# The load of q split into 120 and 8 partitions, in an attention kernel with routed adapters

## The chip, the cores and the metric

The kernel runs on one core of one Trainium2 chip. The metric is device time in microseconds; smaller is better. The core has five engines that run their own queues of instructions: PE (TensorE, matrix products), DVE (VectorE), ACT (ScalarE), POOL (GpSimd) and SP (SyncE). Here SP issues nearly all transfers, and 16 DMA engines carry them out.

## What is computed

There are 4 batches of 8 heads with 768 positions of 64 values. Each position of q and k is hashed into a bucket by the signs of six projections. Attention is allowed only between positions of the same bucket. The result, brought to 3072 rows of 512, goes through a small mixture of adapters: each row takes its two best of eight experts, each of rank 16, and adds what they give.

```python
q_bits = (np.einsum('bhsd,dk->bhsk', q, proj) > 0)
k_bits = (np.einsum('bhsd,dk->bhsk', k, proj) > 0)
mask = q_bucket[:, :, :, None] == k_bucket[:, :, None, :]
scores = np.where(mask, scale * np.matmul(q, k.transpose(0, 1, 3, 2)), -1e9)
attn = softmax(scores)
x = (attn @ v) as (B * S, H * D)
logits = x @ w_gate                     # top 2 of 8, softmax over them
out = x + sum over the two experts e of w_e * (x @ A[e]) @ B[e]
```

## The kernel before

The work is cut into 16 pairs of heads (`N`, counted from 0). A pair has six slots. In each slot PE computes one stretch of scores, 128 x 1536, into one of two buffers (`score`, line 265), and ACT takes the exponential of it (line 286); 96 such exponentials are the backbone of the run. The rest of each slot is other work for earlier and later pairs, written out by hand in `work` (line 691). Every engine runs its list in exactly that order.

What is done for one pair p, and when:

- **Loads.** `loadqk` (line 144) loads q (i = 0) or k (i = 1) of a pair, both heads at once: 128 partitions, two runs of 384 floats in each, 384 KB. From pair 2 on, pair p issues q of pair p + 4 in slot 2, directly ahead of v of pair p + 2 (`loadv`), and k of pair p + 4 in slot 4. The tiles `nat` have four buffers. The first loads are issued in `start` (pairs 0 to 2), `first` (pairs 3 and 4) and pair 1's slots.
- **Hashing.** `turn32` (line 175, instruction on line 180) transposes q or k of one head in blocks of 32 on DVE, `hash` multiplies with the projections on PE, `sign` (line 205) makes signs `sg` on DVE, `signs_out` (line 212) stores them to DRAM as `dr`, and `signs_in` (lines 220 and 224) loads them back in another order, into rows 64 to 71 of `aug`. A bucket match thereby becomes part of the score's matrix product.
- **q and k for the scores.** `natcast` (line 232) casts `nat` to bf16 on POOL. q goes through PE (`trq`) and DVE (`qcopy`, line 247) into `aug`; k of most pairs goes through a transposing transfer (`turnk`, line 253). `shift` (line 261) copies the second head's half on POOL.
- **After the scores.** `pvk` (line 303) multiplies with v on PE, `norm` (lines 321 and 323) divides on DVE and writes `x`, `to_bf` (line 332) casts on POOL to `xb`, and `turn` (line 338) transposes it by a transfer into `xT`.
- **Adapters.** In some pairs, called routing pairs here, `lgz`, `route1`, `route_exp`, `gates` (lines 434 and 436) compute the routing and `zm` for three tiles, and `zt_dma` (line 489) transposes `zm` by a transfer into `zT`. In the pair behind, `delta` multiplies on PE (`dl`, line 503) and adds on DVE (`acc`, line 524), and `store` writes to the output (line 533).

In the steady part SP therefore issues for each pair, in this order: q, v, the store of signs (dr), xT, in routing pairs zT, k, in some pairs output stores, the signs' load (aug<-dr), and k's transpose (aug<-nb). An issue that has to wait holds up all that stand behind it on SP. SP's and ACT's transfers share eight completion semaphores in turn, so an issue also waits until the transfer eight issues before it has landed.

The readers of the q part of `nat` are `turn32` on DVE, two for each pair, and `natcast` on POOL, one for each pair.

Of the kernel before, what the change touches and what calls it, by code (L numbers as in the profile page):

```python
# [19 lines left out]
class Emitter:  # L20
# [123 lines left out]
    def loadqk(self, p, i, h=None, eng=None):  # L144
        if p >= self.N:
            return
        eng = eng or self.nc.sync
        if p not in self.nat:
            self.nat[p] = self.natp.tile([self.P, 2, 2, self.T * self.D], F32, tag="nat", name=f"nat{p}")
        s = self.src((self.q, self.k)[i], p)  # L150
        if h is None:
            eng.dma_start(out=self.nat[p][:, i], in_=s)
        else:
            eng.dma_start(out=self.nat[p][:, i, h], in_=s[:, h])
# [811 lines left out]
```

## Time and profile before

| | us |
|---|---|
| median of 3 runs | 167.91 |
| the three runs | 171.59, 167.91, 166.63 |
| the profiled execution | 167.42 |
| its span, first to last instruction | 165.6 |

The span is 1.8 us shorter than the execution's own time. The views quoted below are of this one execution. In the table of engines a name is followed by busy time, share of the span and number of instructions; PEld is PE's loading of weights, which overlaps its products. The slices cut the span into 40 equal parts with the busy share in tenths. In the groups and waits an arrow points from what was awaited to who waited. In a timeline a line has its start, its length, the engine, the line of the kernel, the operation, the tiles as out<-in, and in brackets the idle time before it with what ended it. In the chain of waits the columns are start, length and what the chain went through; a name such as SPq is the issuing queue of an engine. The granted clock of PE was 0.986 on average.

### The profile page before, as it was taken

How to read it: one execution, taken by the hardware profiler on the slowest of the kernel's cores; microseconds unless marked ns; L12 is line 12 of the kernel's file. 1: busy time of each engine (PE TensorE's matmuls, PEld its weight loads, DVE VectorE, ACT ScalarE, POOL GpSimd, SP SyncE). 2: the span in 40 equal slices, each digit the busy share in tenths (PEclk: the TensorE clock that was granted, in tenths of full speed). 3: DMA queues.
4: the chain of work that ended last, by engine and by line, in shares of the span. 5: the costliest groups of instructions: out<-in, count | busy, mean ns of one | idle time of the engine just before them, and what ended most of it. 6: DMA issues, size and time to landing. Idle time of an engine off the chain costs nothing.

```text
span 165.6 us, 5300 instructions
## 1 busy us (share of the span) xinstructions
PE 149.5 (90%) x2148; PEld 101.8 (61%) x2148; DVE 110.4 (67%) x290; ACT 143.6 (87%) x122; POOL 110.4 (67%) x164
## 2 busy tenths in 40 slices
PE   6787998997999999999998999899999999999840
PEld 2244675675666666666765677576756666879500
DVE  5786895554747699486858696659766545656770
ACT  3466989798999999899998999989999999998640
POOL 3688969696878879694979397948976742510060
PEclk9999999999999999999999999999999999999995
DMA  5874659999999999999989999999998950439036
GB/s 146 279 246 117 199 125 205 260 237 224 169 202 190 211 190 241 185 214 340 256 178 254 321 255 155 251 247 285 174 245 153 248 94 4 86 124 294 6 132 248
DMA packets 58331, 33.09 MB, mean 200 GB/s; under 512 B 43714, under 2 KB 56002, under 8 KB 58306
## 3 DMA queue, kind: packets, MB, share of 16 engines
q1 hardware_dynamic: 57632, 32.46, 89.0%
q8 instruction: 17, 0.28, 0.7%
q10 hardware_dynamic: 674, 0.29, 0.6%
q14 instruction: 8, 0.07, 0.2%
HBM read 20.18 MB, written 7.05 MB: 164 GB/s over the span
## 4 chain that ended last, share of the span: by engine, by line
PE 49%; DMA 20%; DVE 16%; POOL 4%; issue 3%; SPq 3%; ACT 1%; DVEq 1%; POOLq 0%
PE s L283 21%; DMA nat<-in_k_dram 13%; PE pv L303 11%; DMA aug<-dr 5%; PE hs L193 4%; DVE R L180 3%; DVE acc L524 3%; PE pv L291 2%; DMA dr<-sg 2%; DVE x L323 2%; PE dl L503 2%; PE tr L241 2%; PE lz L405 2%; DVE gw L434 2%; DVE zm L436 1%
## 5 line engine op out<-in xcount | busy, mean ns | idle before, releaser
L286 ACT ACTIVATE P<-s 128x1536 bf16<-128x1536 f32 x96 | 135.3, 1450 | 11.3 <-PE s L283 9.0
L283 PE MATMUL s<-aug 71*128 71x512 bf16 (+2 forms) x432 | 78.5, 308 | 4.2 <-DMA aug<-dr 3.0
L283 PEld LDWEIGHTS <-aug 71*128 71x128 bf16 x432 | 34.2, 97 | 25.6 <-issue 8.0
L303 PEld LDWEIGHTS <-P 128*128 128x128 bf16 x1080 | 41.7, 98 | 7.2
L303 PE MATMUL pv<-vb,P 128*128 128x65 bf16 x1080 | 44.3, 193 | 0.0
L180 DVE STREAM_TRANSPOSE R<-nat 128x384 f32<-128x384 f32 x62 | 33.3, 560 | 5.8 <-DMA nat<-in_k_dram 4.9
L261 POOL COPY aug<-aug 64x768 bf16<-64x768 bf16 x30 | 24.8, 827 | 16.3 <-issue 11.1
L232 POOL CAST nb<-nat 128x768 bf16<-128x768 f32 x30 | 24.8, 828 | 2.0 <-DMA nat<-in_q_dram 0.7
L332 POOL CAST xb<-x 128x768 bf16<-128x768 f32 x15 | 12.4, 824 | 15.1 <-issue 6.5
L247 DVE TENSOR_SCALAR aug<-tr 128x768 bf16<-128x768 bf16 x20 | 11.0, 555 | 14.5 <-issue 6.5
L323 DVE TENSOR_TENSOR x<-pv,ri 128x384 f32<-128x384 f32 x30 | 16.7, 557 | 1.0
L170 POOL TENSOR_TENSOR vs<-vn 128x384 f32<-128x384 f32 x16 | 15.9, 996 | 0.0
L193 PE MATMUL hs<-R,hst 128*32 128x192 f32 x248 | 15.4, 332 | 0.2 <-DVE R L180 0.2
L524 DVE SCALAR_TENSOR_TENSOR acc<-dl,rt,x 128x512 f32<-128x512 f32 x18 | 13.3, 738 | 1.6 <-PE dl L503 1.6
L168 POOL CAST vb<-vn 128x768 bf16<-128x768 f32 x16 | 13.3, 828 | 0.2 <-DMA vn<-in_v_dram 0.2
L205 DVE TENSOR_SCALAR sg<-hs,ssc 128x192 bf16<-128x192 f32 (+1 forms) x17 | 7.1, 418 | 8.4 <-PE hs L193 8.4
L193 PEld LDWEIGHTS hs<-R,hst 128*32 128x32 f32 x248 | 7.2, 109 | 7.7 <-issue 2.5
L321 DVE RECIPROCAL ri<-pv 128x6 f32<-128x6 f32 x30 | 5.5, 184 | 9.4 <-PE pv L303 9.4
L291 PE MATMUL pv<-vb,eps 128*128 128x390 bf16 x30 | 10.1, 337 | 1.2 <-DVE x L323 0.6
L241 PE MATMUL tr<-ident_bf,nb 128*128 128x128 bf16 x120 | 10.0, 219 | 0.0
L241 PEld LDWEIGHTS <-nb 128*128 128x128 bf16 x120 | 8.4, 97 | 2.6
L522 POOL TENSOR_TENSOR acc<-acc,x 128x512 f32<-128x512 f32 x2 | 2.5, 1266 | 9.8 <-ACT acc L521 9.8
(111 smaller groups left out, 107.0 us busy)
## 6 DMA issues: line engine op xcount, KB each, us to landing
vn<-in_v_dram SPq DMA_DIRECT2D x16, 384.0 KB, 6.3
nat<-in_q_dram SPq DMA_DIRECT2D x15, 384.0 KB, 5.2
nat<-in_k_dram SPq DMA_DIRECT2D x15, 384.0 KB, 5.1
out_dram<-acc SPq DMA_DIRECT2D x7, 512.0 KB, 3.5
out_dram<-acc SPq DMA_DIRECT2D x9, 256.0 KB
dr<-sg SPq DMA_DIRECT2D x14, 48.0 KB, 5.0
aug<-dr SPq DMA_DIRECT2D x14, 48.0 KB
nat<-in_q_dram SPq DMA_DIRECT2D x2, 192.0 KB
```

The lines of the kernel that those rows point to most:

```text
L170: nc.gpsimd.tensor_add(out=s3, in0=vn[:, :, 0:3, :], in1=vn[:, :, 3:6, :])
L180: self.nc.vector.transpose(out=self.R[p][:, i, h, :], in_=self.nat[p][:, i, h, :])
L193: nc.tensor.matmul(out=hs[32 * j:32 * j + 32], lhsT=self.hst[:, hf].rearrange("p b i -> p (b i)"), rhs=rhs, start=(hf == 0), stop=(hf == 1 ...
L232: self.nc.gpsimd.tensor_copy(out=self.nb[p][:, i].rearrange("p t h d -> p h t d"), in_=self.nat[p][:, i].rearrange("p h (t d) -> p h t d", ...
L241: self.nc.tensor.transpose(out=tr[:, t, :], in_=self.nb[p][:, i, t].rearrange("p h d -> p (h d)"), identity=self.ident_bf)
L261: self.nc.gpsimd.tensor_copy(out=a[0:64, :, 2 + i, :], in_=a[64:128, :, i, :])
L283: nc.tensor.matmul(out=ps[:, o:o + w].rearrange("p (t c) -> p t c", c=P), lhsT=aug[0:71, kt, 2 * h + 1, :], rhs=rhs, start=True, stop=True)
L286: nc.scalar.activation(out=self.P_[p][:, s * W:end], in_=ps, func=ACT.Exp, scale=128.0)
L291: self.nc.tensor.matmul(out=pv, lhsT=self.eps, rhs=self.vb[p % 3][:, h, T:T + 1, :].to_broadcast([self.P, T, D + 1]), start=True, stop=Fal ...
L303: self.nc.tensor.matmul(out=pv[:, i, :], lhsT=self.P_[p][:, o:o + P], rhs=vb[:, h, kt, :], start=False, stop=(kt == T - 1), skip_group_che ...
L323: nc.vector.tensor_tensor(out=self.x[b][:, :, c:c + D], in0=pv[:, :, 0:D], in1=ri.unsqueeze(2).to_broadcast([P, T, D]), op=ALU.mult)
L524: nc.vector.scalar_tensor_tensor(out=out, in0=ps, scalar=rt, in1=self.x[b][:, i, :], op0=ALU.mult, op1=ALU.add)
```

## The change

q of a pair is loaded as before for pairs 0, 1 and 2. From pair 3 on (p > 2), which is the fourth, the load of both heads is issued as two transfers on the same queue, one right behind the other: partitions 0 to 119 and partitions 120 to 127. That is 360 KB and 24 KB in place of 384 KB, for 13 of the 16 pairs. k, v and all else stay, and the order of the instructions on PE, DVE, ACT and POOL is unchanged. What reads q waits for both transfers.

```diff
         s = self.src((self.q, self.k)[i], p)
-        if h is None:
+        if h is None and i == 0 and p > 2:
+            for r in (slice(0, 120), slice(120, 128)):
+                eng.dma_start(out=self.nat[p][r, i], in_=s[r])
+        elif h is None:
             eng.dma_start(out=self.nat[p][:, i], in_=s)
         else:
             eng.dma_start(out=self.nat[p][:, i, h], in_=s[:, h])
```

`src` (line 140) gives the part of q in DRAM with the 128 partitions outermost, so `s[r]` are the same partitions.

## The prediction

> **What bounds the kernel now.** I read the table of engines, the slices, the waits of ACT and PE, and then the chain of waits around each gap.
>
> ```profile
> PE 149.5 (90%) x2148; PEld 101.8 (61%) x2148; DVE 110.4 (67%) x290; ACT 143.6 (87%) x122; POOL 110.4 (67%) x164
> DMA  5874659999999999999989999999998950439036
> q1 hardware_dynamic: 57632, 32.46, 89.0%
> q8 instruction: 17, 0.28, 0.7%
> 16.00:152.00 136.00, 130.83 (x2000) 92.36 (x1997) 92.04 (x228) 129.54 (x99) 97.44 (x131) 1.00 0.99 205
> ```
>
> The last line is the steady part: length, then PE, PEld, DVE, ACT and POOL busy, clock and DMA share. ACT, which runs the exponentials, is busy 129.54 of 136.00 us. If every transfer became free, no more than 136.00 − 129.54 = 6.5 us could go there, and much of that is small change between exponentials. The DMA engines are full as well (9 in nearly every slice, 0.99 here), so a transfer can push another back. The timeline of ACT shows where it waited:
>
> ```profile
> 39.36 22.69 ACT L286 ACTIVATE P<-s 128x1536 bf16<-128x1536 f32 x16 [0.69 <-PE s L283]
> 90.27 7.33 ACT L286 ACTIVATE P<-s 128x1536 bf16<-128x1536 f32 x5 [0.54 <-PE s L283]
> 108.08 7.33 ACT L286 ACTIVATE P<-s 128x1536 bf16<-128x1536 f32 x5 [0.60 <-PE s L283]
> ```
>
> Three of these gaps lead back to transfers. At 39.36 it is the signs coming back (aug<-dr, issued at 32.15, 6.25 us long). At 90.27 and 108.08 it is a load of k that DVE waits for: k, then the transposes R, then acc, then PE's dl.
>
> ```profile
> 30.37 0.57 SPq L152
> 31.00 0.46 SPq L152
> ...
> 32.15 6.25 DMA aug<-dr
> 38.44 0.82 PE s L283 x4
> ...
> 83.44 4.02 DMA nat<-in_k_dram
> 87.48 1.04 DVE R L180 x2
> 88.52 0.64 DVE acc L524
> 89.20 0.38 PE dl L503
> ...
> 100.78 4.50 DMA nat<-in_k_dram
> ```
>
> **q itself is not late.** DVE's transposes waited for k, hardly for q:
>
> ```profile
> DVE R L180 <- DMA nat<-in_k_dram: 4.9, 7, 1.0
> DVE R L180 <- DMA nat<-in_q_dram: 0.7, 1, 0.7
> nat<-in_q_dram SPq DMA_DIRECT2D x15, 384.0 KB, 5.2
> ```
>
> A q load lands 5.2 us after issue. It is issued in slot 2 of a pair and first read, by turn32 of its first head, in slot 1 of the next: five of six slots of a period of 8.9 us (DVE's signs start at 68.80 in one pair and at 77.68 in the next; their rows are below), 7.4 us. So nothing is won by q landing sooner, and in the steady part a q that lands 1 us later still lands in time. What can count is what the edit does to SP's queue and to the other transfers.
>
> **The change, part by part.** Thirteen loads (pairs 3 to 15) become two issues each: 120 partitions, then 8. No byte and no arithmetic instruction is added, and the order of every engine's instructions stays, except for the 13 issues on SP.
>
> *SP's time.* The nearest row to a load of 8 partitions is the sign load, also 8 partitions wide:
>
> ```profile
> L224 SPq DMA_DIRECT2D aug<-dr x6: 283/298/350, 12.7 to 22.3; - x6
> L152 SPq DMA_DIRECT2D nat<-in_q_dram x15: 373/582/919, 2.7 to 112.2; - x15
> ```
>
> The lower end is its 0.30 us, the upper end the 0.58 us of a whole q load; I take 0.30 plus 0.05 between two issues, 0.35 us, since width is what the nearest row shares. The first part stays at 0.58. In all 13 × 0.35 = 4.6 us of SP time. Where does it lie on the path?
>
> (a) At 30.37 SP issues q, k, one piece of the adapter weights and then the sign load for which PE waits, one right behind the other. The added issue stands ahead of it: +0.35 us. At worst +0.58; at best about 0.1, if the 6.25 us of that load are mostly time behind other packets.
>
> (b) In the pairs that route (zT), SP runs q, v, dr, xT, zT, k.
>
> ```profile
> 59.65 0.92 SPq L152 DMA_DIRECT2D nat<-in_q_dram  x1
> ...
> 61.12 1.53 SPq L212 DMA_DIRECT2D dr<-sg  x1
> 62.76 1.23 SPq L338 DMA_TRANSPOSE xT<-xb  x1
> 64.08 1.20 SPq L489 DMA_TRANSPOSE zT<-zm  x1
> 63.16 0.56 DVE L436 TENSOR_TENSOR zm<-lz,gw 128x384 bf16<-128x384 f32 x1
> ```
>
> In the first of them zT waits for SP (xT ends at 63.99, zm had ended at 63.72), so up to 0.35 us goes on to k at 65.33. I take 0.2, because dr took 1.53 us there against 0.37 elsewhere: an issue that stalls for full queues absorbs time ahead of it.
>
> (c) In the other pairs SP waits for sg or for an engine behind v, which covers it:
>
> ```profile
> 77.42 0.45 SPq L160 DMA_DIRECT2D vn<-in_v_dram  x1
> 78.12 0.37 SPq L212 DMA_DIRECT2D dr<-sg  x1
> 78.59 3.35 SPq L338 DMA_TRANSPOSE xT<-xb  x1
> 82.03 1.36 SPq L489 DMA_TRANSPOSE zT<-zm  x1
> 68.80 0.42 DVE L205 TENSOR_SCALAR sg<-hs,ssc 128x192 bf16<-128x192 f32 x1 [0.68 <-PE hs L193]
> 77.68 0.42 DVE L205 TENSOR_SCALAR sg<-hs,ssc 128x192 bf16<-128x192 f32 x1 [0.24 <-PE hs L193]
> ```
>
> v ends at 77.87, dr waits for sg until 78.10: 0.23 of the 0.35 us is hidden here, the rest by the stall in xT. If that cover went, each routing pair would pay up to 0.35.
>
> *Waits.* The semaphores of SP's transfers are used in turn, eight of them, so an issue waits for the eighth one before it; with 13 more, that one was issued a little later. Eight issues fill nearly a period of 8.9 us and a load lands in about 5, so the eighth before has landed as a rule. Where issues are densest, behind 32 us, one may have to wait, but what stands behind it there (v, dr, xT) is not what PE waits for. The readers of q (turn32 on DVE, natcast on POOL) now wait for two landings. That is one semaphore more in an instruction, or a separate wait instruction, on engines busy 67% of the time: nothing on the path.
>
> *The share of the DMA engines.* Here the edit can win. xT took 1.23 us to issue at 62.76 and 3.35 at 78.59, though its source was ready (the cast to xb had ended at 78.38, so the profile's naming of later POOL work as releaser is a coincidence of time). The long ones have an instruction packet beside them:
>
> ```profile
> 77.56 0.82 POOL L332 CAST xb<-x 128x768 bf16<-128x768 f32 x1 [0.33 <-DVE x L323]
> L338 SPq DMA_TRANSPOSE xT<-xb x15: 1227/1773/3348, 28.7 to 147.7; - x15
> q8 instruction: 1, 0.02, 1.9%
> 80.97 0.56 DVE L436 TENSOR_TENSOR zm<-lz,gw 128x384 bf16<-128x384 f32 x1
> ```
>
> The q8 row is from the window 78.6 to 82; the window of the short xT, 62.7 to 64.1, has none. Seventeen such packets took 0.7% of 16 × 165.6 us, 1.09 us each, and one packet is on one engine. An engine that stops for 1.1 us fills up, and I read the stretched xT as SP unable to hand that engine more. A q load's share of one engine is of the same size: 32.46 MB took 89.0% of 165.6 us, 4.54 us per MB, so 0.39 MB is 1.8 us by the mean over all transfers, and less for loads alone. [...] Its worth on the path: at 78.59 xT would end near 79.9 in place of 81.94, zT would then wait only for zm, which ended at 81.53, and k goes out 0.45 us earlier, inside the 0.54 us gap at 90.27: −0.45. In the next such pair the stall buys nothing at the issue:
>
> ```profile
> 96.33 2.66 SPq L338 DMA_TRANSPOSE xT<-xb  x1
> 99.30 1.42 SPq L489 DMA_TRANSPOSE zT<-zm  x1
> 98.72 0.56 DVE L436 TENSOR_TENSOR zm<-lz,gw 128x384 bf16<-128x384 f32 x1
> ```
>
> zm ends at 99.28 and zT starts at 99.30, not when xT ends (98.99). A somewhat emptier queue ahead of k is worth 0 to 0.6 there (the gap at 108.08); I take −0.2.
>
> No row shows over how many engines 120 partitions go. [...]
>
> *Sum.* +0.35 + 0.2 − 0.45 − 0.2 = −0.1 us on the profiled execution, 167.42 us (span 165.6). That execution lies between the lowest and the median of the three times (166.63, 167.91, 171.59). I forecast 167.3 us, no change that a measurement tells: 2% of 167.9 is 3.4 us, about what separates a difference from none on this kernel.
>
> **Rivals.** *Slower, the wide part is badly spread (0.17).* If 120 partitions do not go over nearly all engines, a q load lasts longer on those it uses: at 8 engines of 15 partitions, 15/8 of its share. With 1.8 us as the share, the mean over all transfers, that adds 7/8 × 1.8 = 1.6 us to each pair of a ring that is 0.99 busy; as loads alone take less, I use 1.1. q can bear it, k behind it cannot: in four routing pairs k would be 1.1 us later, 4 × 1.1 = 4.4 us, 167.4 + 4.4 = 171.8. For it speaks that the ring has no idle stretch left to absorb it; against it that SP, not the ring, sets when k is issued. It decides once k lands more than about 1 us later than the 4.0 to 4.5 us of now.
>
> *Faster, the spared engine is what holds everything (0.12).* [...]
>
> *The spared engine is another (0.13).* [...]
>
> **The numbers.** The forecast holds 0.58, with 166.2 to 168.6 for the unknown prices and the scatter of a median of three. Half of the fast rival passes 2% and some noise joins it: faster 0.10. Most of the slow rival and the same noise: slower 0.17. Within 2%: 0.73. For 8 in 10 I go from 165.0, which leaves out the fast rival's lower half, to 171.0, which leaves out the slow rival's upper part.
>
> **What would show it.** q's row of 384 KB becomes one of 360 and one of 24; the issue of the 24 near 0.30 us. Right: the longest xT falls from 3.35 towards 1.3 to 2, zT at the routing pairs starts right behind zm, ACT's gap near 90 shrinks, that near 39 grows by 0.1 to 0.5. Wrong: xT as long as before (another engine spared), k landing later than 4.5 us (bad spread), or DVE's R waiting for q. A gain above 3 us would mean that ACT lost time to transfers in places where I saw only small change.

## The result and the profile after

The changed kernel takes 180.83 us, the median of four runs (179.40 to 182.24), beside 167.55 us for the kernel before on the same chip. The ratio is 1.084 with an interval of 1.077 to 1.090, so 13.3 us are lost. The forecast was 167.3 us. Runs of one kernel spread by some us here, and the long ones show a lower mean granted clock (0.931 in the longest of these four, 0.949 in the shortest); ratios leave those out, and the medians below hold all runs.

The profiled execution, the longest of the four, took 182.24 us with a span of 180.4. Below stand from its page the engines' busy time, the granted clock in 40 slices, the share of q1, the queue of SP's transfers that is called the ring here, and the exponentials (last part: idle time of ACT ahead of them and what ended most of it):

```profile
PE 158.1 (88%) x2147; PEld 106.6 (59%) x2148; DVE 110.3 (61%) x290; ACT 143.9 (80%) x122; POOL 110.4 (61%) x164
PEclk9997599997599999999999999956999999999995
q1 hardware_dynamic: 57723, 32.46, 90.2%
L289 ACT ACTIVATE P<-s 128x1536 bf16<-128x1536 f32 x96 | 135.6, 1452 | 25.7 <-PE s L286 23.7
```

ACT works as long as before (143.9 against 143.6 us). The group's idle time was 11.3 us before and is 25.7 now: these 14.4 us are nearly all of the span's 14.8. ACT waits for the scores of PE, and PE shows something that was not there: three places at half clock (a granted clock of 0.5) ahead of the tail. Who PE and DVE wait for stands in the view of waits (us in total, times, longest):

```profile
DVE R L183 <- DMA nat<-in_k_dram: 8.0, 5, 3.6
PE dl L506 <- DVE acc L527: 6.5, 4, 3.3
PE s L286 <- DMA aug<-dr: 4.5, 2, 2.7
DVE R L183 <- DMA nat<-in_q_dram: 4.1, 4, 2.3
```

R's wait for k was 4.9 us with a longest of 1.0; now one alone takes 3.6. R's wait for q was 0.7 us in all. The chain that ended last, cut to the two kinds of place (start, duration, what):

```profile
35.69 6.96 DMA aug<-dr
...
42.70 1.43 PE s L286 x4
...
84.90 6.52 DMA nat<-in_q_dram
...
91.45 0.58 DVE R L183
...
92.08 5.12 DMA nat<-in_k_dram
...
97.23 1.04 DVE R L183 x2
98.27 0.65 DVE acc L527
...
98.95 0.38 PE dl L506
```

The sign load took 6.25 us and takes 6.96; k took 4.02 and takes 5.12; a q load of 6.52 us is on the chain, where none was. (The chain goes from this q to k by R; but SP's issue of zT ended at 92.03 as R did, so that q held up the issue of k is not shown.) PE idles 2.67 us ahead of 42.70 and 2.87 ahead of 98.95, and at 119.41, by the same path behind a k of 5.79 us, 3.27. What this does to ACT shows in windows (start and end, length, then PE, PEld, DVE, ACT and POOL busy, granted clock, DMA share, GB/s):

```profile
42.00:51.00 9.00, 8.30 (x75) 5.23 (x76) 2.45 (x7) 4.22 (x3) 4.86 (x8) 0.62 1.21 173
51.00:98.00 47.00, 44.33 (x670) 30.74 (x669) 31.09 (x78) 44.99 (x35) 36.32 (x49) 1.00 1.14 204
98.00:104.00 6.00, 5.03 (x73) 3.46 (x72) 4.31 (x9) 3.98 (x3) 1.73 (x3) 1.00 1.14 299
117.90:124.60 6.70, 5.20 (x38) 3.07 (x38) 4.10 (x8) 2.32 (x2) 1.65 (x2) 0.50 1.14 286
```

Between 51 and 98 us ACT is busy 96% of the time. At that rate the three other windows lack 4.4, 1.8 and 4.1 us of ACT, 10.3 of the 14.8. Most of the rest lies at the start: a wait of 1.85 us for signs at 14.91 and a half clock behind it. That sign load was issued ahead of the first divided q. The same wait is 1.02 us in the kernel before and anything from none to 1.92 us in the runs below, so it is not explained by the change.

### The profile page after: what moved, and what is told of

It reads as the page before. It is cut to its first block, busy times and chain, and to the rows that moved or that the text cites. A ratio compares the mean times of both kernels' runs of the same rounds, so it can differ in the third digit from the quotient of the medians.

```text
span 180.4 us, 5333 instructions
## 1 busy us (share of the span) xinstructions
PE 158.1 (88%) x2147; PEld 106.6 (59%) x2148; DVE 110.3 (61%) x290; ACT 143.9 (80%) x122; POOL 110.4 (61%) x164
## 3 DMA queue, kind: packets, MB, share of 16 engines
q1 hardware_dynamic: 57723, 32.46, 90.2%
## 4 chain that ended last, share of the span: by engine, by line
PE 59%; DMA 22%; DVE 11%; issue 2%; ACT 1%; SPq 1%; DVEq 1%; POOL 0%; POOLq 0%
PE s L286 26%; PE pv L306 14%; DMA nat<-in_k_dram 9%; DMA nat<-in_q_dram 6%; PE hs L196 5%; DMA aug<-dr 5%; PE pv L294 3%; PE tr L244 3%; DMA dr<-sg 3%; DVE R L183 3%; PE dl L506 3%; DVE acc L527 2%; DVE x L326 2%; PE lz L408 2%; ACT P L289 1%
## 5 line engine op out<-in xcount | busy, mean ns | idle before, releaser
L289 ACT ACTIVATE P<-s 128x1536 bf16<-128x1536 f32 x96 | 135.6, 1452 | 25.7 <-PE s L286 23.7
L286 PE MATMUL s<-aug 71*128 71x512 bf16 (+2 forms) x432 | 83.2, 321 | 5.7 <-DMA aug<-dr 4.5
L286 PEld LDWEIGHTS <-aug 71*128 71x128 bf16 x432 | 35.3, 100 | 34.0 <-issue 14.2
L306 PEld LDWEIGHTS <-P 128*128 128x128 bf16 x1080 | 44.3, 101 | 8.3 <-issue 1.6
L306 PE MATMUL pv<-vb,P 128*128 128x65 bf16 x1080 | 46.7, 198 | 0.0
L527 DVE SCALAR_TENSOR_TENSOR acc<-dl,rt,x 128x512 f32<-128x512 f32 x18 | 13.3, 739 | 1.8 <-PE dl L506 1.8
L506 PE MATMUL dl<-Bcat,zT 128*128 128x512 bf16 x18 | 7.2, 403 | 6.5 <-DVE acc L527 6.5
L294 PE MATMUL pv<-vb,eps 128*128 128x390 bf16 x30 | 10.7, 357 | 1.4 <-DVE x L326 0.8
L244 PEld LDWEIGHTS <-nb 128*128 128x128 bf16 x120 | 9.0, 102 | 3.0 <-issue 0.6
L244 PE MATMUL tr<-ident_bf,nb 128*128 128x128 bf16 x120 | 10.7, 228 | 0.0
```

Source lines behind the costliest of these rows:

```text
L244: self.nc.tensor.transpose(out=tr[:, t, :], in_=self.nb[p][:, i, t].rearrange("p h d -> p (h d)"), identity=self.ident_bf)
L286: nc.tensor.matmul(out=ps[:, o:o + w].rearrange("p (t c) -> p t c", c=P), lhsT=aug[0:71, kt, 2 * h + 1, :], rhs=rhs, start=True, stop=True)
L289: nc.scalar.activation(out=self.P_[p][:, s * W:end], in_=ps, func=ACT.Exp, scale=128.0)
L294: self.nc.tensor.matmul(out=pv, lhsT=self.eps, rhs=self.vb[p % 3][:, h, T:T + 1, :].to_broadcast([self.P, T, D + 1]), start=True, stop=Fal ...
L306: self.nc.tensor.matmul(out=pv[:, i, :], lhsT=self.P_[p][:, o:o + P], rhs=vb[:, h, kt, :], start=False, stop=(kt == T - 1), skip_group_che ...
L527: nc.vector.scalar_tensor_tensor(out=out, in0=ps, scalar=rt, in1=self.x[b][:, i, :], op0=ALU.mult, op1=ALU.add)
```

## The experiments

All losses below are differences of medians, beside the runs of the kernel before on the same chip in the same session (167.1 to 168.5 us).

**What a load costs by itself.** A kernel that only loads q, in nine forms, whole q twice: each form four times alone, then eight in a row.

> This kernel only loads parts of q and writes zeros; the rest of the computation is left out, so its time says nothing of the other kernels'. Each form (128, 120, 112, lower 64, upper 64, 8 partitions, 120+8, 112+16, 64+64, and 128 again) is loaded four times with a wait after each, and eight times without. Theory A (the 120 partitions are so laid on the DMA engines that they take about twice as long as 128, by 0.9 us in the changed kernel): without waits a 120-partition load costs 1.8 to 2.1 us against 1.0 to 1.3 for 128; 112 partitions, shared differently, stay near 1.0 to 1.4. Rival B (it is the added issue on SP's queue and the semaphores, not the data): 120 and 112 cost the same as 128 within 10%, and 120+8 costs at most one issue (0.35 us) more. Rival C (any split or any half-filled set of engines is slow): 112 and 64 are slow too for their bytes.

DVE reads each load of a row as it lands, so the starts' spacing is the time that one load holds the ring. In the timeline of DVE, two loads of 128 partitions, then two of 120, then two pairs of 120 and 8:

```profile
24.42 0.17 DVE L68 COPY z<-many 128x8 f32<-128x8 f32 x1 [0.84 <-DMA many<-in_q_dram]
25.47 0.17 DVE L68 COPY z<-many 128x8 f32<-128x8 f32 x1 [0.88 <-DMA many<-in_q_dram]
...
49.49 0.17 DVE L68 COPY z<-many 128x8 f32<-128x8 f32 x1 [1.41 <-DMA many<-in_q_dram]
51.06 0.17 DVE L68 COPY z<-many 128x8 f32<-128x8 f32 x1 [1.40 <-DMA many<-in_q_dram]
...
171.94 0.17 DVE L68 COPY z<-many 128x8 f32<-128x8 f32 x1 [1.70 <-DMA many<-in_q_dram]
173.75 0.17 DVE L68 COPY z<-many 128x8 f32<-128x8 f32 x1 [1.65 <-DMA many<-in_q_dram]
```

Once its row runs evenly, a whole q holds the ring 1.02 to 1.05 us (the first spacings of each such row hold one of 2.2 us), 120 partitions of it 1.57 to 1.58, the pair 1.8 to 1.9. So fewer bytes take half as long again as all bytes. Alone, 112 partitions take about 1.35 us, 64 take 0.96 and 8 about 0.5. Of the other pairs, 112 and 16 take 1.6 us, 64 and 64 take 1.60. This rules out rival B; 120 stays below theory A's 1.8 to 2.1, and 64 is slow for its bytes, as rival C had it. So the change adds some 13 × 0.75 = 9.8 us of ring time, an estimate from these spacings.

The ring carried 57632 packets before, 57723 in the changed kernel, and in the kernel with two halves, which comes below:

```profile
q1 hardware_dynamic: 57840, 32.46, 86.6%
```

That is 91 and 208 more, 7 and 16 for each divided load, with the same bytes. Over how many engines a transfer goes stands in no trace.

**The ring's time or the second transfer.** Three kernels in one session. One keeps q whole and adds a load of its last 8 partitions that nobody reads; two divide q elsewhere.

```diff
+            if i == 0 and p > 2:
+                eng.dma_start(out=self.x8, in_=s[120:128])
```

> The kernel before with one more transfer behind each q load from pair 3 on: the 8 partitions 120 to 127 again, into a tile that nobody reads. [...] Theory A: within 1% of before, 166.5 to 169 us. Rival B: the same loss as the change, 178 to 182 us.

```diff
-            for r in (slice(0, 120), slice(120, 128)):
+            for r in (slice(0, 112), slice(112, 128)):
```

> The change with 112 and 16 partitions in place of 120 and 8. Theory A (the way 120 rows fall on the engines): most of the loss is gone, 166.5 to 171 us. Rival B (issue and semaphores): 178 to 182 us. Rival C (any split): 175 to 182 us.

```diff
-            for r in (slice(0, 120), slice(120, 128)):
+            for r in (slice(0, 64), slice(64, 128)):
```

> The change with 64 and 64 partitions. [...] Theory A in the form that only a number of partitions that does not fill 16 engines is slow: 166.5 to 170 us. Rival B: 178 to 182 us, as 64+64 has the same number of issues.

The added load: 171.59 us against 168.47, with ten runs from 167.23 to 178.15, and a ratio of 1.002 (0.994 to 1.010). So SP's second issue and its semaphores cost nothing by the ratio and some 3 us by the medians, far from the 178 to 182 us of rival B. The division at 112: 174.45 us, ratio 1.038 (1.017 to 1.059). In halves: 179.18 us, ratio 1.067 (1.051 to 1.084), not the 166.5 to 170 us of theory A. The division into even and odd partitions below carries the same 57840 packets and lost a third as much, so that count does not decide.

**Divided by head.** Two transfers of 128 partitions each.

```diff
-            for r in (slice(0, 120), slice(120, 128)):
-                eng.dma_start(out=self.nat[p][r, i], in_=s[r])
+            for r in range(2):
+                eng.dma_start(out=self.nat[p][:, i, r], in_=s[:, r])
```

> Two transfers per q as in the changed kernel, from the same pairs on, but split by head: each takes all 128 partitions. [...] Theory B (two transfers in place of one cost by themselves: two issues, two sets of semaphore updates, two waits for R): close to the changed kernel, 176 to 182 us, ratio over 1.05.

Measured 171.21 us against 167.09 (four runs, 167.20 to 172.06, beside 166.27 to 170.53). The loss is 4.1 us in the median and none in the shortest run: below the 176 to 182 us of theory B, and far from the changed kernel. The profiled execution, of 171.88 us, has a wait of dl for acc of 2.8 us. That two transfers as such cost anything is not shown; they bring at most 4 of the 13 us, the way in which they are cut the rest.

**Where it is lost.** The change for pairs 3 to 6 alone, and for pairs 7 on alone.

```diff
-        if h is None and i == 0 and p > 2:
+        if h is None and i == 0 and 2 < p < 7:
```

> The 120 and 8 split for pairs 3 to 6 alone. Theory A: the wait of s for aug<-dr near 42 us stays (over 2 us) with its stretch at half clock, those of dl near 99 and 119 us go: about half of the 13 us lost is left, 172 to 176 us, ratio 1.03 to 1.05. Rival (one place decides and the rest follows from it): either 168 or 180.

```diff
-        if h is None and i == 0 and p > 2:
+        if h is None and i == 0 and p > 6:
```

> The 120 and 8 split for pairs 7 on alone. Theory A: nothing is lost before 60 us, the waits of dl for acc behind R and k stay (2.5 us and more, with k landing 5 us and more after its issue): 172 to 176 us, ratio 1.03 to 1.05, and together with the kernel that splits only pairs 3 to 6 the losses add up to the 13 us of the changed kernel within 3 us. Rival: either 168 or 180.

170.15 us (ratio 1.020, 1.012 to 1.029) and 176.84 us (1.056, 1.045 to 1.067), both against 167.09: 3.1 and 9.8 us, 12.8 together, as the sum was expected; the shares were not. Per divided load that is 0.8 and 1.1 us. In the profiled execution of the first kernel PE's wait for the signs near 42 us is 0.90 us, not the expected 2 and more; its half clock lies at the start, behind the wait of 1.92 us that stands ahead of every divided load, so what the first four cost is shown by the times and not by a place. The waits of the second kernel show where:

```profile
L183 DVE STREAM_TRANSPOSE R<-nat 128x384 f32<-128x384 f32 x62 | 33.2, 559 | 10.3 <-DMA nat<-in_k_dram 9.1
L506 PE MATMUL dl<-Bcat,zT 128*128 128x512 bf16 x18 | 7.2, 402 | 5.1 <-DVE acc L527 5.0
```

R waits 9.1 us for k, and PE's dl 5.0 us for acc behind it, as in the changed kernel (8.0 and 6.5).

**k ahead of the transposes.** The changed kernel, with k's load issued before xT and zT.

```diff
+            if p > 1:
+                add(3, "loadqk", n4, 1)
             if not last:
                 add(3, "turn", p - 1)
...
-            add(4, "loadqk", n4, 1)
+            if p == 1:
+                add(4, "loadqk", n4, 1)
```

> The changed kernel with k of each pair from the sixth on issued on SP ahead of xT and zT instead of behind them. Theory A (R waits for k because q, v, dr, xT and zT stand before it in the rings): R no longer waits for k, the waits of dl near 99 and 119 us go, the wait near 42 us may stay: 171 to 176 us. Rival (the rings are full, so that xT and zT are late instead and PE waits in the gate products): 178 us or more.

171.78 us (167.61 to 172.50) against 167.09: with the same transfers on the ring, about 9 of the 13 us are back. Some 2 of these 9 come from moving k by itself, as the kernel before with the same edit shows below. The waits:

```profile
DVE R L183 <- DMA nat<-in_q_dram: 6.0, 5, 2.2
PE s L286 <- DMA aug<-dr: 4.3, 3, 2.9
PE dl L506 <- DMA zT<-zm: 2.2, 3, 0.9
DVE R L183 <- DMA nat<-in_k_dram: 2.1, 2, 2.0
PE dl L506 <- DVE acc L527: 0.2, 1, 0.2
```

dl's wait for acc has gone from 6.5 to 0.2 us, R's for k from 8.0 to 2.1. The wait for the signs is left, and one for zT is new but short. Measured against the kernel before with k moved as well, the change still costs some 7 us here ((171.78 − 167.09) + (167.46 − 165.32), medians of two sessions). So about half of its loss hangs on k standing last in the order behind a q that got longer.

**As much ring time without dividing q.** The kernel before with a second load of 64 partitions behind each q.

```diff
+            if i == 0 and p > 2:
+                eng.dma_start(out=self.x64, in_=s[64:128])
```

> The kernel before, q whole, and behind each q from pair 3 on a second load of its last 64 partitions into a tile that nobody reads: the rings carry about 2.0 us per q (1.05 and 0.95, from the kernel of loads) where the changed kernel's pair of transfers carries 1.8. R waits for no second part. Theory A (what costs is the time on the rings, by whatever transfer): as slow as the changed kernel, 176 to 186 us. Rival (the cost hangs on q's own second part, that R and the cast wait for it): 168 to 172 us.

183.11 us against 167.46, ratio 1.089 (1.073 to 1.106). Here also 13 × 192 KB more are read, which the change does not do.

```profile
DVE R L183 <- DMA nat<-in_k_dram: 13.6, 8, 3.9
PE dl L506 <- DVE acc L527: 7.2, 3, 3.6
PEclk9999999997999999955899999956999999999995
```

q is whole and lands first, nobody waits for the added load, and the kernel is as slow as the changed one, by the same waits and with half clock at three places as well. The time on the ring suffices as the cause, whichever transfer takes it.

**The kernel before with k earlier.** The same edit to the schedule as above, q whole.

> The kernel before, q whole, with k of each pair from the sixth on issued on SP ahead of xT and zT. Theory A: R's waits for k (4.9 us in the sum of its group) go, xT and zT land later by about the ring time of a k: 165 to 168 us, 0.98 to 1.00. Rival (xT and zT late cost more): 169 us or more.

165.32 us (163.63 to 169.42) against 167.46, ratio 0.980 (0.975 to 0.985), the shortest of all kernels here, faster than both. The profiled execution is the longest of its four, 169.42 us.

```profile
DVE R L180 <- DMA nat<-in_k_dram: 3.1, 3, 1.1
PE dl L503 <- DVE acc L524: 0.2, 1, 0.2
```

R's wait for k fell from 4.9 to 3.1 us, not to nothing; dl waits for acc no more than 0.2.

**Which partitions.** Only loads again.

> Only loads of q, all else left out, the output zeros. Time on the rings of one load, from the spacing of landings in a row of eight. [...] Rival (any transfer that isn't all 128 partitions is slow, whichever they are): the even 64 0.96 like the lower 64, and even and odd together 1.6.

From the timeline of DVE: lower 64 partitions, even 64, pairs of lower and upper half, pairs by head.

```profile
46.71 0.17 DVE L70 COPY z<-many 128x8 f32<-128x8 f32 x1 [0.74 <-DMA many<-in_q_dram]
47.67 0.17 DVE L70 COPY z<-many 128x8 f32<-128x8 f32 x1 [0.78 <-DMA many<-in_q_dram]
...
71.23 0.17 DVE L70 COPY z<-many 128x8 f32<-128x8 f32 x1 [0.41 <-DMA many<-in_q_dram]
71.97 0.17 DVE L70 COPY z<-many 128x8 f32<-128x8 f32 x1 [0.56 <-DMA many<-in_q_dram]
...
177.12 0.17 DVE L70 COPY z<-many 128x8 f32<-128x8 f32 x1 [1.49 <-DMA many<-in_q_dram]
178.76 0.17 DVE L70 COPY z<-many 128x8 f32<-128x8 f32 x1 [1.47 <-DMA many<-in_q_dram]
...
231.98 0.17 DVE L70 COPY z<-many 128x8 f32<-128x8 f32 x1 [0.86 <-DMA many<-in_q_dram]
233.03 0.17 DVE L70 COPY z<-many 128x8 f32<-128x8 f32 x1 [0.88 <-DMA many<-in_q_dram]
```

Over a whole row (first to last landing, divided by seven) the lower 64 take 0.92 us and the even 64 take 0.76, with spacings from 0.49 to 0.95; lower and upper half take 1.64, even and odd 1.43 with one spacing of 2.1, the last two of that row 1.0. The even 60 of the first 120 take 1.00. For whole q and for the pairs by head this measure is spoilt by a single long spacing near the start of the row (2.6 to 3.0 us; 1.30 and 1.26 with it); the steady spacings behind it are about 1.05 for both. 96 partitions take 1.04.

SP needed 5.16 us to issue the eight transfers of the even 64, 7.52 for the even 60, and 10.35 for the sixteen of even and odd: 0.65, 0.94 and 1.29 us for each load or pair. So the even rows stand near the end that SP sets, and a mean under 0.65 us for the even 64 could not have shown itself. The halves, with 10.34 us, do not stand there. The rival's 0.96 us for the even 64 and 1.6 for even and odd together did not come. It is shown that 64 neighbouring partitions take nearly as long as all 128 (0.92 us beside 1.05), and that the same number spread out takes less (0.76). Which memory this comes from is not shown, for the addresses in DRAM change together with the partitions.

**Which partitions, in the kernel.** The same two issues of 64, cut into even and odd.

```diff
-            for r in (slice(0, 120), slice(120, 128)):
+            for r in (slice(0, 128, 2), slice(1, 128, 2)):
```

> The changed kernel with q cut into its 64 even and its 64 odd partitions. SP issues the same two transfers of 64 partitions as in the kernel with lower and upper half (179.2 us), and waits and updates are the same. In the kernel of loads a row of such pairs landed every 1.0 to 1.3 us where lower and upper half took 1.64. Theory A (which partitions neighbour each other decides how long q keeps the rings busy, and that decides the loss): 168 to 173 us. Rival (two transfers of less than 128 partitions are slow whichever they are, or SP's two issues of 0.6 us decide): 176 to 182 us.

171.58 us (ten runs, 168.66 to 175.88) against 167.96, ratio 1.016 (1.009 to 1.022), where the halves had 1.067. SP's work is the same in both (most pairs take it 1.26 to 1.3 us to issue), so some 7 us hang on which partitions a transfer takes.

**Half clock, in the kernel.** Matmuls by zeros, added onto pv, to keep PE busy ahead of dl.

```diff
+    def fill(self, p):
+        pv = self.pv[p, 0]
+        for n in range(14):
+            self.nc.tensor.matmul(out=pv, lhsT=self.wz[:, 0:128],
+                                  rhs=self.wz[:, 0:390].rearrange("p (t d) -> p t d", t=6),
+                                  start=False, stop=False, skip_group_check=True)
...
+            if p in (10, 12) and s == 3:
+                add(s, "fill", p)
             add(s, "delta", d, i)
```

> The changed kernel, and in the two pairs where dl waited 2.87 and 3.27 us for acc 14 matmuls by a weight of zeros, added onto pv ahead of the first dl, that fill some 2.2 us of the wait and change no sum. Theory A with the clock (the waits cost what they last, and again as much because PE then runs some 6.8 us at half clock): the stretch at half clock near 118 us goes, 174 to 178 us. Rival (the clock follows from elsewhere, the waits alone are the cost): 180 to 183 us, with the stretch at half clock still there.

180.16 us (177.09 to 184.63) against 167.46; the second pair was the wrong one (dl had waited in the ninth and the eleventh), so this tells little.

```diff
-            if p in (10, 12) and s == 3:
+            if p in (8, 10) and s == 3:
...
-        for n in range(14):
+        for n in range(6):
```

> The changed kernel with 6 matmuls by zeros, 0.33 us each as the first such kernel showed, so 2.0 us, added onto pv ahead of the first dl of the two pairs (the ninth and the eleventh) in which dl waited 2.87 and 3.27 us. The first try put 4.6 us into the eleventh and the thirteenth pair. Clock counts beside the waits: the mean clock of its runs rises from 0.93 to 0.95 to over 0.95, 175 to 179 us. Rival (only the waits cost): 180 to 183 us; a rise of the clock without a shorter time would speak for the rival too.

The expectation has a wrong price: a matmul lasts 0.33 us, but six of them overlap and took 1.16 us. The time was 179.91 us, ratio 1.071 (1.060 to 1.083), and the mean clock of the four runs 0.954, beside 0.941 of the changed kernel's four. In the profiled runs the stretches at half clock ahead of the tail last 3 × 3.4 us where they lasted 3 × 6.8. The time lies between the two ranges that were expected, 175 to 179 and 180 to 183. By the expectation's last sentence the rise of the clock with 1 us gained speaks for the rival, that the waits are the cost; but late data put waits of 1.5 to 2.7 us elsewhere, so the two parts are not separated.

**Half clock, by itself.** Bursts of matmuls between waits of known length.

> None of the reference's work, the output zeros: bursts of 64, 69 and 74 matmuls of 512 columns on PE, each behind a wait for a chain of 1 to 7 clears on DVE (0.48 us each), so that PE idles some 1 to 4 us, three times each. If a wait of 2 us and more brings half clock by itself: stretches of 6.8 us (or 3.4) at 0.5 behind most waits of 2 us and more, none behind those of 1 us, and matmuls of twice the duration in them. [...]

From the timeline of PE: start and length of a burst, its matmuls, and in brackets the wait ahead of it.

```profile
49.80 13.99 PE L49 MATMUL burst<-w 128*128 128x512 bf16 x62 [2.14 <-DVE w L57]
66.58 13.99 PE L49 MATMUL burst<-w 128*128 128x512 bf16 x63 [2.80 <-DVE w L57]
84.03 15.67 PE L49 MATMUL burst<-w 128*128 128x512 bf16 x63 [3.46 <-DVE w L57]
...
176.03 15.06 PE L49 MATMUL burst<-w 128*128 128x512 bf16 x67 [2.14 <-DVE w L57]
193.90 16.75 PE L49 MATMUL burst<-w 128*128 128x512 bf16 x68 [2.80 <-DVE w L57]
...
309.76 3.60 PE L49 MATMUL burst<-w 128*128 128x512 bf16 x10 [2.15 <-DVE w L57]
313.58 14.01 PE L49 MATMUL burst<-w 128*128 128x512 bf16 x62 [0.22 <-issue]
330.39 17.83 PE L49 MATMUL burst<-w 128*128 128x512 bf16 x73 [2.80 <-DVE w L57]
```

In each round the bursts behind waits of 0.8 and 1.5 us have the shortest length (13.99, 15.07, 16.15 us). Behind 2.8 us the burst is as short once and 1.68 us longer twice; behind 2.15 us it is longer once in three (the rows at 309.76 and 313.58 are one burst); behind 3.46 us and more in all nine. So half clock followed twelve of the fifteen waits of over 2 us and none of the six of 0.8 and 1.5 us, as was expected; of the six from 2.14 to 2.80 us it followed three. A wait of 2 to 3 us thus brings half clock or not; what decides is not shown. The stretches last 3.41 and 6.83 us here, and one of 3.4 us costs PE 1.7 us more.

## Why the prediction failed

**The ring time of a divided q.** The sum held no term for it. Only the rival "Slower, the wide part badly spread" did, and it tied the slowness to the number of engines, which no trace shows. By the loads above 120 partitions hold the ring 1.57 us against 1.05 for 128, and 64 hold it 0.92. This missing term, some 0.75 us for each divided load, is the step that failed: with as much ring time and q left whole, the loss came back in full (183.11 us). Why 120 partitions take longer is open. It is shown that it matters which partitions a transfer takes: the lower 64 took 0.92 us, the even 64 0.76, all 128 1.05. Why neighbouring ones take longer, and why 120 take longer than 128, no run tells.

**"A q that lands 1 us later still lands in time."** It did not: R waited 0.71 us for q at 91.45 and 0.59 at 111.40 (4.1 in all, 2.3 of it behind the dense issues at 33 us), and the first of these q landed 6.52 us after its issue where 5.2 was usual. The prediction counted slots, 7.4 us from issue to first read. In the kernel before, the q issued at 76.79 was read 6.42 us later, so little more than 1 us was to spare in the routing pairs:

```profile
83.21 0.57 DVE L180 STREAM_TRANSPOSE R<-nat 128x384 f32<-128x384 f32 x1
```

Still, this was not the main loss; with k moved ahead R waited 6.0 us for q, and 9 us were won.

**The rival's size.** It had the course of the loss, a longer q and a later k, and the point from which it decides: k landing over 1 us later than 4.0 to 4.5 us. k landed 5.12 and 5.79 us after issue, 1.10 and 1.29 more than before. Each load was priced at 1.1 us of ring time, more than the 0.75 that the loads show, and the whole at 4 routing pairs × 1.1 = 4.4 us; the loss was 13.3. Three things are missing. The first four divided loads, of which the rival took no account, already cost 3.1 us. A late k was taken to delay PE by its later landing alone, while it was also issued later, as the paragraph on the relief shows: PE's waits for acc grew from 0.59 and 0.65 us to 2.87 and 3.27. And nothing was set down for PE's clock behind such waits. Its chance of 0.17 and the upper end of 171.0, below that rival's own 171.8, were too low in any case.

**SP's time, +0.35 and +0.2.** The price of one more issue was right where SP was not held up: a divided q takes it 0.95 us at 84.90, a whole one took 0.58 at 76.79. With the added load of 8 the issues cost nothing by the ratio (1.002). Two transfers by head, which hold the ring about as long as one, lost 4.1 us in the median and even and odd 3.6, more than these terms, but the shortest run by head lost nothing. At the sign load behind 32 us the sum had +0.35, and PE's wait there went from 1.03 to 2.67 us: the sign load is issued 2.57 us after the q ahead of it where it was 1.78 (33.12 to 35.69, before 30.37 to 32.15), and takes 0.71 us more to land.

**The relief, −0.45 and −0.2.** It did not come; SP got later instead. Both terms suppose a DMA engine that the edit relieves, and no run shows one; what the runs showed in its place is k issued 1.18 and 1.33 us later. At these two places zT was to start right behind zm, and k behind zT. But zm ends at 88.99, and SP is busy with xT until 90.30:

```profile
88.43 0.56 DVE L439 TENSOR_TENSOR zm<-lz,gw 128x384 bf16<-128x384 f32 x1
90.39 1.64 SPq L492 DMA_TRANSPOSE zT<-zm  x1
```

k, at 92.08, is issued 3.09 us behind the end of zm where it was 1.91, and at the next place, 111.87, 2.83 where it was 1.50: 1.18 and 1.33 us later. With the later landing, 1.10 and 1.29 us, that makes 2.28 and 2.62, just what PE's waits grew by. So half of the lateness arose on SP, ahead of k's issue, and half on the ring, behind it. xT's longest issue rose from 3.35 to 4.34 us:

```profile
L341 SPq DMA_TRANSPOSE xT<-xb x15: 1210/1788/4342, 31.9 to 162.3; - x15
```

That was the prediction's own sign of being wrong. The 17 instruction packets are there as before, with 0.8% of 16 engines' span where they had 0.7%.

**What stays open.** How the loss divides between waits and half clock. Three stretches of 6.83 us can cost PE up to 3 × 3.4 us, but the third begins at 117.9, in a wait that ends at 119.41, and the filled waits did not settle it. That one wait of 2.87 us had no half clock behind it and still lacked 1.8 us of ACT shows that the waits cost by themselves.

## What to carry to other kernels

Price a divided transfer by the time that each part holds the ring, measured in a row of its own kind, not by its bytes: neighbouring partitions in less than all 128 can be slower than the whole (120 took 1.57 us, 128 took 1.05). On a ring as full as this one (q1 took 90.2% of 16 engines' span), ask which load stands last in the issue order and has a reader waiting; the same edit cost 13 us with k behind the transposes and about 7 with k ahead of them, and moving k alone made the kernel before faster. A later issue and a later landing of such a load add up. Where PE's waits come near 2 us, count that the clock may fall behind them; half clock followed twelve of the fifteen waits of over 2 us above.

## What the runs showed of the hardware that was not expected

A load of 120 partitions of 3 KB each holds the ring 1.57 us, one of 128 holds it 1.05. Half clock comes in stretches of 3.41 us or two or three times as long (10.24 with the added load of 64), and may follow waits of 2.15 us or leave out waits of 2.80. The ring's count of packets rises by 7 for each q divided into 120 + 8 and by 16 for each divided into halves, by head, or into even and odd.
